# Two transposed inputs of a fused attention and feed-forward kernel, made in another stretch of the program

## The chip, the core and the metric

The kernel runs on one core of a Trainium2 chip. The metric is the time of one execution in microseconds (us), as the device measures it. Profiled executions come with a trace, in which PE is TensorE (matmuls), DVE VectorE, ACT ScalarE, POOL GpSimd and SP SyncE; SP and POOL here mostly issue DMA transfers.

## What is computed

```python
def _attn_ref(q, k, v):                      # (8, 12, 448, 64)
    scores = scale * np.matmul(q, k.transpose(0, 1, 3, 2)) - np.log(S)
    attn = 1.0 / (1.0 + np.exp(-scores))
    return np.matmul(attn, v).astype(np.float32)

def _moe_ref(x, w_in, w_out):                # (3584, 768), (768, 2048), (2048, 768)
    h = x @ w_in
    g = h * (1.0 / (1.0 + np.exp(-h)))
    return (g @ w_out).astype(np.float32)
```

The attention has a sigmoid in place of a softmax, so no row has to be normalised. Its output, with the heads of a token side by side, is the x of the second part: a hidden layer with `h * sigmoid(h)`, and an out layer. Inputs and output are float32; the kernel computes in float16 and adds up in float32.

## The kernel before

**Tiles of the attention.** Four heads of one batch make a *quad*; a batch has three, and there are 24: quads 0 to 2 are batch 0, quads 6 to 8 batch 2, quads 9 to 11 batch 3. The 448 tokens of a quad are cut into seven rounds, so a batch has 21 units `(quad, round)`. For a quad, `load` (L78) brings q and k from memory as float16 rows (`qf`, `kf`, four buffers each) and v (`vf`, three buffers), by transfers that POOL issues. Scores need q and k transposed (`qT`, `kT`, four buffers each). For quads 0 to 5 TensorE transposes them. From quad 6 on it is done by `dma_transpose` (L164): one copy puts the rows in order (`kr` or `qr`, three buffers each), and a transfer from SP's queue transposes them into `kT` or `qT`. `scores` does the scores of one unit, a TensorE stage of four matmuls and a sigmoid on ScalarE. `values` (L232, L243) multiplies a whole quad's attention with v and puts the result into `xT`.

**The second part.** A batch's hidden layer (`moe_h`) has 16 blocks (`h_unit`) of six matmuls, a sigmoid and a product on VectorE. In the out layer, two row blocks make one `out_set`: by a Strassen-like scheme it takes seven products of eight matmuls each (56 in all) in place of eight products. Before, between and after these, VectorE makes sums of the inputs (`S`, L350 to L360) and adds up the products (`osb`, L346); the weights' sums (`T`, L308) are made once, during batch 1's hidden layer and two of them in the first set. The output goes out by SP's queue, from two of the four `osb` buffers for each set. Products, hidden blocks, values and the scores' "single" banks share four PSUM banks (`ps_1`).

**The order.** Everything is issued in the order of the program text, with no scheduler. The second part is one long stream of steps, each a matmul with what belongs to it: hidden layers of batches 0 and 1, sets (0, 0), (0, 2) and (0, 4), hidden layer of batch 2, and so on. A generator (`all_moe`) hands them out. The attention runs beside it in bursts: `burst` issues the scores of two or three units, then `values_if_any`, then `rows_if_any`; then `stretch` takes steps from the stream until they have filled a given time. In `stretch`, when half of it is done, `rows_if_any` is called once more. So behind the first units of batch 2 come steps of set (0, 0), and so on.

**The steps that the change touches.** `after_values` (L496) runs when a quad's values have been issued. It loads v for three quads on and, for quads from 6 on, puts quads into the list `later`, k and q as two entries. `rows_if_any` (L435) takes one entry from the list: it issues the copy on VectorE, the transpose on SP's queue and, behind a q, the load of q and k four quads on, which takes the buffers that have just been copied. Before the change, batch 2's first values (quad 6) put quads 9 and 10 into the list, so four entries are taken by four calls; quads 7 and 8 put in 11 and 12. Quads 6, 7 and 8 are copied by ScalarE within batch 1's hidden layer (`by_h1`), after which POOL waits for the transpose of q of quad 8 (`gate`, L403) and loads quads 10, 11 and 12. Quad 9 is loaded behind quad 5's values. `moe_set` (L407) runs through the steps of a set with an index `i` from 0 to 55 and can put something behind a step; in set (0, 0) these are the last two pieces of the weights' sums, behind 10 and 14.

Of the kernel before, what the change touches and what calls it, by code (L numbers as in the profile page):

```python
# [17 lines left out]
def kernel(  # L18
# [9 lines left out]
    nc = tc.nc  # L28
# [13 lines left out]
    NQB = NQ * B  # L42
# [24 lines left out]
    def new_flat(name, g):  # L67
        flat[name, g] = (p3 if name == "v" else p4).tile(
            [P, 2, NCH, D], F16, tag=f"{name}f", name=f"{name}f"
        )  # L70

    def rows_in(name, g):
        b, iq = divmod(g, NQ)
        return source[name][b, 4 * iq : 4 * iq + 4].rearrange(
            "(i h) (p c) d -> (h p) i (c d)", h=2, c=NCH
        )

    def load(names, g, c0=0, c1=NCH):  # L78
        for name in names:
            if (name, g) not in flat:  # L80
                new_flat(name, g)
            nc.gpsimd.dma_start(  # L82
                flat[name, g][:, :, c0:c1].rearrange("p i c d -> p i (c d)"),
                rows_in(name, g)[:, :, c0 * D : c1 * D],
            )
# [22 lines left out]
    def load_w_in(step):  # L108
        cols = slice(step * DFF // 4, (step + 1) * DFF // 4)
        rows = moe_w_in[:, cols].rearrange("(iq j h d) f -> h j d iq f", j=2, h=2, d=D)  # L110
        for half in range(2):
            for j in range(2):
                nc.gpsimd.dma_start(
                    w_in_sb[j * D : (j + 1) * D, half * NQ : (half + 1) * NQ, cols], rows[half, j]
                )

    def load_w_out(nh, part):
        cols = slice(nh * NO2, (nh + 1) * NO2)
        fcs = slice(part * NFC // 2, (part + 1) * NFC // 2)
        nc.gpsimd.dma_start(  # L120
            w_out_sb[:, fcs, cols],
            moe_w_out[part * DFF // 2 : (part + 1) * DFF // 2, cols].rearrange(
                "(fc p) e -> p fc e", p=P
            ),
        )
# [3 lines left out]
    def new_qkT(g):  # L129
        for name in ("k", "q"):  # L130
            qkT[name, g] = p4.tile([P, NCH, P], F16, tag=f"{name}T", name=f"{name}T")
# [32 lines left out]
    def dma_transpose(g, name, copy):  # L164
        if ("k", g) not in qkT:
            new_qkT(g)
        rows = p3.tile([P, NCH, 2, D], F16, tag=f"{name}r", name=f"{name}r")
        copy(rows, flat[name, g].rearrange("p j c d -> p c j d"))  # L168
        nc.sync.dma_start_transpose(
            out=qkT[name, g], in_=rows.rearrange("p c j d -> p (c j d)")  # L170
        )
# [141 lines left out]
    def block(g):  # L313
        return gTr[:, :, g * P : (g + 1) * P]

    def row_blocks(m, g):
        return [rows_of[2 * m + u // NCH, u % NCH] for u in (2 * g, 2 * g + 1)]
# [89 lines left out]
    def moe_set(m, g):  # L407
        step = out_set(block(g), row_blocks(m, g), block(g + 1), row_blocks(m, g + 1))
        for i, ns in enumerate(step):
            if m % 2 == 0 and g == 2 and i % 8 == 4 and i < 32:  # L410
                fcs = slice(i // 8 * 4, i // 8 * 4 + 4)
                nc.scalar.activation(kept[:, fcs], block(NCH - 1)[:, fcs], AF.Copy)  # L412
            if m == 0 and g == 0 and i in (10, 14):
                next(sums)
            yield ns

    def all_moe():
        for m in range(B // 2):
            yield from moe_h(2 * m)
            if m > 0:  # L420
                yield from moe_set(m, 0)
            yield from moe_h(2 * m + 1)
            if m == 0:
                yield from moe_set(m, 0)
            yield from moe_set(m, 2)
            yield from moe_set(m, 4)
            if m % 2 == 1:
                g = NCH - 1
                yield from out_set(
                    kept, row_blocks(m - 1, g), block(g), row_blocks(m, g), m == B // 2 - 1  # L430
                )

    later = []

    def rows_if_any():  # L435
        if later:
            g, name = later.pop(0)
            dma_transpose(g, name, nc.vector.tensor_copy)
            if name == "q" and g + 4 < NQB and g + 4 > 12:
                load("kq", g + 4)  # L440

    stream = all_moe()
# [2 lines left out]
    def stretch(ns):  # L445
        nonlocal done, due
        due = max(due + ns, done + 0.75 * ns)
        middle = due - ns / 2
        since = 0
        while done < due or hold:  # L450
            step_ns = next(stream, None)
            if step_ns is None:
                break
            done += step_ns * weight
            since += step_ns
            if since > 1300:
                late_sigmoid()
            if done > middle:
                rows_if_any()
                middle = math.inf  # L460
        late_sigmoid()
# [34 lines left out]
    def after_values(g):  # L496
        if g == 0:
            load("v", 3)
            load_w_in(2)
            load_w_in(3)  # L500
        elif g == 1:
            load("v", 4)
            load_w_out(0, 0)
            load_w_out(0, 1)
        elif g == 2:
            load("v", 5)
            load_w_out(1, 0)
            load_w_out(1, 1)
            load("kq", 6)
            load("kq", 7)  # L510
        elif g + 3 < NQB:
            load("v", g + 3)
        if g == 5:
            load("kq", 9)
        if g >= 6:
            for to in (9, 10) if g == 6 else (g + 4,):
                if to < NQB:
                    later.extend(((to, "k"), (to, "q")))

    def values_if_any():  # L520
        if waiting:
            g = waiting.pop(0)
            values(g)
            after_values(g)
# [17 lines left out]
    def rounds(g, end):  # L542
        values(g, end)
        if end == NCH:
            after_values(g)
# [37 lines left out]
    def burst(n, tiles):  # L583

        new = units[n : n + (tiles if not waiting else 2)]
        for i, u in enumerate(new):
            single = i == len(new) - 3
            scores(*u, single_banks() if single else None, len(new) == 3 and i == 2)
        values_if_any()
        rows_if_any()  # L590
        waiting.extend(g for g, ch in new if ch == NCH - 1)
        return len(new)
# [51 lines left out]
```

## Time and profile before

| | us |
|---|---|
| three runs | 382.36, 381.93, 381.32 |
| their median | 381.93 |
| the profiled execution, its own time | 378.82 |
| its span in the trace | 377.1 |
| granted TensorE clock, mean | 0.998 |

The span runs from the first to the last recorded instruction; the execution's own time is 1.7 us more. In the 40 slices of the page, each 9.4 us long, a digit is the busy share in tenths and 9 is 90% or more. The copies that are moved lie in the tenth and eleventh slice:

```profile
PE   7999999999999999999999999999999999999995
DVE  2555646997766466548576557645675457556773
DMA  8999999987999909919599734435062300210333
```

Where these stages lie in the trace: batch 1's hidden layer ends at 76.3 us, set (0, 0) runs from there to 87.7, with bursts of scores within it at 78.5, 82.1 and 85.6 (three units each). The values of quad 6 are at 89.6, those of quad 7 at 97.2 and those of quad 8 at 108.5. The first unit of quad 9 is the last of the three in the burst at 104.5.

In the lines of a timeline below, the columns are the start and the duration in us, the engine, the line of the kernel, the operation, what is written and read, shapes, and how many instructions are merged; in brackets stands how long the engine was idle before and what ended that.

### The profile page before, as it was taken

The numbers are of one execution on the slowest core, as the hardware profiler recorded it, in microseconds if no ns is written. First come the engines' busy times: TensorE is split into PE (matmuls) and PEld (weight loads), VectorE is DVE, ScalarE is ACT, GpSimd is POOL, SyncE is SP. The second block draws the span as 40 slices with busy tenths as digits, with TensorE's granted clock in tenths as the row PEclk, the third lists the DMA queues.
The fourth block names the chain that finished last, engine by engine and source line by source line (L and its number), as shares of the span: only waits on it lengthen the run. The fifth ranks groups of instructions, "written<-read, shape, count | busy, mean of one in ns | idle before, by whom it ended". The sixth has DMA issues, their size and how long they took to land.

```text
span 377.1 us, 7624 instructions
## 1 busy us (share of the span) xinstructions
PE 368.9 (98%) x3081; PEld 189.5 (50%) x3081; DVE 234.0 (62%) x417; ACT 243.3 (65%) x355; POOL 66.1 (18%) x99
## 2 busy tenths in 40 slices
PE   7999999999999999999999999999999999999995
PEld 3544445555554455455555545544555455555663
DVE  2555646997766466548576557645675457556773
ACT  5998885778777776676556676667866685243000
POOL 8565523042412002102120200000000000000000
PEclk9999999999999999999999999999999999999999
DMA  8999999987999909919599734435062300210333
GB/s 137 198 204 204 205 203 203 177 122 153 136 164 223 216 2 120 160 50 108 73 161 193 108 101 75 55 104 75 0 144 41 85 2 2 52 31 2 83 85 83
DMA packets 65698, 42.79 MB, mean 113 GB/s; under 512 B 36096, under 2 KB 62208, under 8 KB 65664
## 3 DMA queue, kind: packets, MB, share of 16 engines
q0 software_dynamic: 27072, 22.58, 41.6%
q1 hardware_dynamic: 38240, 19.44, 28.4%
q8 instruction: 24, 0.39, 0.4%
q10 hardware_dynamic: 352, 0.30, 0.2%
q14 instruction: 10, 0.08, 0.1%
HBM read 45.61 MB, written 11.01 MB: 150 GB/s over the span
## 4 chain that ended last, share of the span: by engine, by line
PE 92%; ACT 6%; issue 1%; DVE 0%; ACTq 0%
PE ph L262 39%; PE po L338 34%; PE psc L196 9%; PE pav L232 8%; ACT attnT L207 5%; PE pw L140 1%; PE ptrq L153 1%; PE ptrk L153 0%; ACT attnT L180 0%; DVE gTr L276 0%; DVE osb L346 0%; ACT kept L412 0%; ACT qT L143 0%; ACT m L353 0%; DVE dummy L476 0%
## 5 line engine op out<-in xcount | busy, mean ns | idle before, releaser
L207 ACT ACTIVATE attnT<-psc,bias_s 128x896 f16<-128x896 f32 (+1 forms) x168 | 138.3, 901 | 45.4 <-PE psc L196 45.2
L262 PE MATMUL ph<-xT,w_in_sb 128*128 128x448 f16 x768 | 151.2, 353 | 0.0
L276 DVE TENSOR_TENSOR gTr<-ph,tsig 128x448 f16<-128x448 f32 x128 | 78.3, 623 | 68.9 <-ACT tsig L274 68.4
L262 PEld LDWEIGHTS <-w_in_sb 128*128 128x128 f16 x768 | 72.8, 98 | 73.6 <-issue 8.2
L274 ACT ACTIVATE tsig<-ph 128x448 f16<-128x448 f32 x128 | 68.4, 549 | 49.1 <-PE ph L262 48.2
L338 PEld LDWEIGHTS <-S 128*128 128x128 f16 x448 | 42.3, 98 | 33.5 <-issue 6.8
L346 DVE SCALAR_TENSOR_TENSOR osb<-po,osb 128x384 f32<-128x384 f32 x70 | 37.6, 554 | 22.4 <-PE po L338 22.1
L196 PE MATMUL psc<-qT,kT 64*64 64x448 f16 x672 | 48.4, 360 | 1.8 <-ACT attnT L207 0.5
L243 DVE TENSOR_SCALAR xT<-pav 128x448 f16<-128x448 f32 x48 | 27.7, 620 | 31.1 <-PE pav L232 31.1
L82 POOL DMA_DIRECT2D vf<-in_v_dram x24 | 17.2, 716 | 166.4 <-PE pav L232 140.3
L338 PE MATMUL po<-T,S 128*128 128x384 f16 x224 | 40.6, 327 | 0.0
L338 PEld LDWEIGHTS <-gTr 128*128 128x128 f16 x304 | 28.7, 98 | 23.5 <-issue 5.4
L338 PE MATMUL po<-w_out_sb,S 128*128 128x384 f16 x224 | 39.9, 326 | 0.0
L232 PE MATMUL pav<-attnT,vf 64*64 64x448 f16 x672 | 38.3, 350 | 0.7 <-DVE gTr L276 0.4
L338 PE MATMUL po<-w_out_sb,gTr 128*128 128x384 f16 x192 | 34.9, 327 | 0.0
L196 PEld LDWEIGHTS <-kT 64*64 64x64 f16 x672 | 16.5, 105 | 29.6 <-issue 25.4
L346 DVE SCALAR_TENSOR_TENSOR osb<-po,m 128x384 f32<-128x384 f32 x42 | 23.2, 553 | 6.2 <-PE po L338 5.1
L232 PEld LDWEIGHTS <-vf 64*64 64x64 f16 x672 | 20.6, 107 | 12.5 <-issue 2.5
L180 ACT ACTIVATE attnT<-psc,bias_s 128x896 f16<-128x896 f32 x26 | 26.6, 1022 | 0.0
L353 ACT ACTIVATE m<-po 128x384 f32<-128x384 f32 x14 | 6.9, 495 | 23.7 <-PE po L338 23.7
L338 PE MATMUL po<-T,gTr 128*128 128x384 f16 x112 | 21.4, 326 | 0.0
L82 POOL DMA_DIRECT2D kf<-in_k_dram x25 | 18.1, 723 | 16.6 <-DVE kr L168 10.3
(43 smaller groups left out, 155.0 us busy)
## 6 DMA issues: line engine op xcount, KB each, us to landing
out_dram<-osb SPq DMA_DIRECT2D x54, 192.0 KB, 2.9
vf<-in_v_dram POOLq DMA_DIRECT2D x24, 224.0 KB, 5.3
kf<-in_k_dram POOLq DMA_DIRECT2D x23, 224.0 KB, 6.5
qf<-in_q_dram POOLq DMA_DIRECT2D x23, 224.0 KB, 7.4
w_in_sb<-in_moe_w_in_dram POOLq DMA_DIRECT2D x16, 192.0 KB, 8.2
w_out_sb<-in_moe_w_out_dram POOLq DMA_DIRECT2D x4, 768.0 KB, 15.4
kT<-kr SPq DMA_TRANSPOSE x18, 6.8
qT<-qr SPq DMA_TRANSPOSE x18, 6.9
```

Of the source, the lines that this page charges most:

```text
L82: nc.gpsimd.dma_start(flat[name, g][:, :, c0:c1].rearrange("p i c d -> p i (c d)"), rows_in(name, g)[:, :, c0 * D : c1 * D],)
L180: nc.scalar.activation(to, psc, AF.Sigmoid, bias=bias_s, scale=QKSCALE)
L196: nc.tensor.matmul(banks[j][own, :S], qkT["k", g][rows, ch, own], qkT["q", g][rows, :, own], start=True, stop=True,)
L207: nc.scalar.activation(to, psc, AF.Sigmoid, bias=bias_s, scale=QKSCALE)
L232: nc.tensor.matmul(pav[half][j * D : (j + 1) * D, :S], flat["v", g][own, j, ch, :], at[own, j, :], start=(ch == 0), stop=(ch == NCH - 1),)
L243: nc.vector.tensor_scalar_mul(xT[b][:, half * NQ + iq, :], pav[half][:, :S], SX)
L262: nc.tensor.matmul(ph[:, :S], w_in_sb[:, cc, fc * P : (fc + 1) * P], xT[b][:, cc, :], start=(at == 0), stop=(at == NCC - 1),)
L274: nc.scalar.activation(tsig, ph[:, :S], AF.Sigmoid, bias=0.0, scale=ISX)
L276: nc.vector.tensor_mul(gTr[:, fc, (b % 2) * S : (b % 2) * S + S], ph[:, :S], tsig)
L338: nc.tensor.matmul(po[:, :NO2], a[:, fc, :], w[:, fc, :], start=(fc == 0), stop=(fc == NHC - 1))
L346: nc.vector.scalar_tensor_tensor(out=o, in0=po, scalar=sign, in1=x, op0=ALU.mult, op1=ALU.add)
L353: nc.scalar.activation(m1, po, AF.Copy, scale=ISX)
```

## The change

```diff
@@ moe_set
             if m == 0 and g == 0 and i in (10, 14):
                 next(sums)
+            if m == 0 and g == 0 and i in (24, 40):
+                dma_transpose(9, "k" if i == 24 else "q", nc.vector.tensor_copy)
+                if i == 40:
+                    load("kq", 13)
             yield ns
@@ rows_if_any
             dma_transpose(g, name, nc.vector.tensor_copy)
-            if name == "q" and g + 4 < NQB and g + 4 > 12:
+            if name == "q" and g + 4 < NQB:
                 load("kq", g + 4)
@@ after_values
         if g >= 6:
-            for to in (9, 10) if g == 6 else (g + 4,):
-                if to < NQB:
-                    later.extend(((to, "k"), (to, "q")))
+            if g + 4 < NQB:
+                later.extend(((g + 4, "k"), (g + 4, "q")))
```

Quad 9's copies and transposes leave the list `later` and are issued in set (0, 0), k behind step 24 and q behind step 40; the load of quad 13 comes right behind the latter. Quad 6's values put only quad 10 into the list, so 10's entries are taken two calls earlier, and quad 14's load is issued with them. The second hunk drops a condition that is true for every quad which comes by there. Matmuls, sigmoids and their order stay as they are, and so does the number of copies, transposes and loads.

## The prediction

> **What bounds the kernel now.** I read the page first (busy times, slices, chain), then the waits of TensorE, then the timeline of each engine from 74 to 112 us, which holds the place the copies go to and the place they leave, then the DMA view there.
>
> ```profile
> span 377.1 us, 7624 instructions
> PE 368.9 (98%) x3081; PEld 189.5 (50%) x3081; DVE 234.0 (62%) x417; ACT 243.3 (65%) x355; POOL 66.1 (18%) x99
> PE 92%; ACT 6%; issue 1%; DVE 0%; ACTq 0%
> ```
>
> TensorE is busy for 98% of the span and the chain of waits runs through it for 92%. Idle are 377.1 - 368.9 = 8.2 us; the slices put most of it in the first (7 tenths) and the last (5 tenths). The list of TensorE's waits holds five, 3.2 us in all:
>
> ```profile
> PE pw L140 <- DVE bias_s L477: 1.5, 1, 1.5
> PE psc L196 <- ACT attnT L207: 0.5, 1, 0.5
> PE psc L196 <- ACT qT L143: 0.5, 1, 0.5
> PE pav L232 <- DVE gTr L276: 0.4, 1, 0.4
> PE pav L232 <- ACT attnT L207: 0.3, 1, 0.3
> ```
>
> By the chain all of them lie before 50 us, and between 57.5 and 137 us TensorE idles for 0.01 us. So in this execution nothing in reach of the change can be made shorter: an edit pays only if it ends a wait that this execution does not show, and costs only if it makes one.
>
> **What is moved, on VectorE.** The copies of quad 9 go into the first set (76.3 to 87.7 us). I count the set's 56 matmuls: 14 lie before the scores at 78.56, 17 before those at 82.12, 17 before those at 85.68. Step 24 is the first matmul of the fourth product, at about 80.9; step 40 is the first of the sixth, at about 84.2. VectorE takes its work in order, so the copy of k stands behind the addition of the third product (82.14) and ahead of the first of the fourth (83.12):
>
> ```profile
> 82.14 0.55 DVE L346 SCALAR_TENSOR_TENSOR osb<-po,m 128x384 f32<-128x384 f32 x1
> 83.12 0.56 DVE L346 SCALAR_TENSOR_TENSOR osb<-po,osb 128x384 f32<-128x384 f32 x1 [0.42 <-PE po L338]
> 83.59 0.55 DVE L346 SCALAR_TENSOR_TENSOR osb<-po,m 128x384 f32<-128x384 f32 x1
> 84.42 0.56 DVE L346 SCALAR_TENSOR_TENSOR osb<-po,osb 128x384 f32<-128x384 f32 x1 [0.28 <-PE po L338]
> 85.72 1.02 DVE L346 SCALAR_TENSOR_TENSOR osb<-po,osb 128x384 f32<-128x384 f32 x2 [0.74 <-PE po L338]
> ...
> 92.17 0.61 DVE L168 COPY kr<-kf 128x896 f16<-128x896 f16 x1
> 92.70 0.61 DVE L168 COPY qr<-qf 128x896 f16<-128x896 f16 x1
> 93.23 0.55 DVE L346 SCALAR_TENSOR_TENSOR osb<-po,m 128x384 f32<-128x384 f32 x1
> ```
>
> The idle time is in brackets. A copy takes 0.61 us and the next instruction starts 0.53 after it (92.17, 92.70, 93.23); an addition costs 0.46 in the same sense (83.59 - 83.12 = 0.47). The copy of k runs from about 82.60 to 83.13, and the addition that came at 83.12 comes at 83.13: cost 0.01 us on VectorE. The copy of q stands behind the fifth product's addition (84.42), runs from 84.88 to 85.41, and the next comes at 85.72 as before. Both are hidden in waits for TensorE of 0.42 and 0.74 us. If that cover is gone, the two delay VectorE by 2 x 0.53 = 1.06 us; late next is a PSUM bank that the next product, or the single banks of the scores at 85.61, must have.
>
> **Behind batch 2's first values** the list then holds 10 alone: its copies take the places of 9's at 92.17 and 92.70, and those at 94.29 and 95.28 vanish. The additions behind these start up to 0.5 us earlier; TensorE waited for none of them (no such row among its waits), so on this trace the gain is 0.00 us. The input of 10 is in place for it: qf of quad 10 is the load issued at 78.53, landing after 5.1 us.
>
> **The queues.** POOL's six loads for 10 to 12 are issued from 77.82 to 82.61; the two for 13, which waited for 9's copies and came at 93.09 and 93.80, now come at about 83.5 and 85.8, and nothing stands behind them until v of quad 9 at 91.41. Those for 14 move from 95.20 and 96.19 to about 93.1 and 93.8. SP's queue:
>
> ```profile
> 86.30 3.21 SPq L331 DMA_DIRECT2D out_dram<-osb  x4
> 92.85 1.23 SPq L169 DMA_TRANSPOSE kT<-kr  x1
> 94.17 1.39 SPq L169 DMA_TRANSPOSE qT<-qr  x1
> 95.67 4.22 SPq L169 DMA_TRANSPOSE kT<-kr  x1
> 99.98 4.09 SPq L169 DMA_TRANSPOSE qT<-qr  x1
> 104.17 4.12 SPq L169 DMA_TRANSPOSE kT<-kr  x1
> ```
>
> The transposes of 9 go ahead of the set's four stores, at about 83.2 and 85.5. At 1.2 to 1.4 us each the stores start up to about 0.6 late; at 4.2 each (the rows from 95.67 on) they start at 91.6 instead of 86.30 and end at 94.8. Their tiles are written again only by the third set, at 106.28. With 5 us to land, the longest median of the stores in this stretch, that leaves over 6 us: cost nothing. The transposes of 10 then follow by about 95 at the latest.
>
> **The one thing that is tight.** The first scores of quad 9 are the third tile of the burst at 104.50:
>
> ```profile
> qT<-qr SPq DMA_TRANSPOSE x1, 10.3
> ...
> 104.50 0.76 PE L196 MATMUL psc<-qT,kT 64*64 64x448 f16 x12
> ```
>
> The first row is the transpose of q for quad 9, issued at 94.17; the last number is its time to landing. It lands at 94.17 + 10.3 = 104.47. The tile's four weight loads start by 104.7, so it had about 0.25 us to spare, by chance. Transposes here take very different times: 6.5 us for k of 9, 13.3 and 13.0 for k and q of 10, against 2.9 at the least in this trace, because they share the 16 engines with POOL's loads for 13, 14 and v. (The Trainium skill's page "DMA: Bandwidth & Descriptors", in "Queues, rings and completion order", says that each DMA engine takes the queues with work in turn, packet by packet. The rows agree: 13.3 us in the jam, 2.9 outside it; by the page a transpose's landing hangs on the loads beside it.) In an execution in which that one transpose takes 0.3 us longer, TensorE stands still in front of the tile, and as it has no slack anywhere, the end moves by what it waits. The price, from the nearest rows: nothing at 10.3 us or less; 94.17 + 13.3 - 104.7 = 2.8 us at the length of the next transpose. After the change this tile's transposes start 9 us earlier and even at 13.3 us land before 99, 6 us early; those of 10 land by about 108, needed at 118.10.
>
> **The sum.** For the profiled execution: 0.0 us, span 377 as before. But this execution's own time was 378.82 (1.7 around its span), and the three runs gave 381.32 to 382.36, median 381.93: 3.1 us more, and 1.04 apart. The trace cannot say what the 3.1 us are. A late qT of quad 9, worth 0 to 2.8 us, is one thing that fits. I take 1.5, about the middle, since the rows on both sides (10.3 and 13.3) are equally near. Forecast 381.93 - 1.5 = **380.4 us**; its own range is 379.0 to 380.7.
>
> **The rivals.** (1) *The transfer is hidden anyway.* The profiled execution speaks for it: no wait, and nothing else in reach. Then the 3.1 us are a matter of the runs that the change doesn't touch: 381.9 us, give or take 0.6. Against it is only that 0.25 us is little beside landings that differ by 7 us.
>
> (2) *VectorE becomes late in the first set.* It has no idle time from 73.7 to 82.7 us, and the copy of k stands right behind that stretch. The place is the fourth product's additions, whose bank TensorE needs between 84.22 (the sixth product's start) and 85.61 (the next single banks); they end at 84.15 now. It decides once they end after that, 0.1 to 1.5 us later. Price: the two copies, 1.06 us, and for each one issue of a POOL load (0.72 us) if the two engines hinder each other, as the copy of k starts when the last of those loads has just been issued (81.89 to 82.61): 1.06 + 1.44 = 2.5 us at most, 383.7 with some 0.7 of it covered by the waits that VectorE has there. Against it: four waits for TensorE in this set, 0.28 to 1.07 us, each of which takes up delay. (The Trainium skill's page "SBUF — State Buffer", in "Who interferes with whom", has a rule against the change: a fast copy of VectorE and an instruction of GpSimd block each other for their whole length. No row here shows it; by it either copy could wait, or the loads for 12 and 13 be late, and these are needed at 111 us and later.)
>
> (3) *The edit is empty*: 9's input not there at step 24. Its loads were issued at 60.82 and 62.01 and took 9.1 and 9.5 us, so they landed by 71.5; this I give no chance.
>
> **How the numbers follow.** Less than 0.3%, 1.15 us, is about what a measurement here can't tell from no change. Forecast 0.46, rival (1) 0.39, rival (2) 0.15. These are the chances of faster, same and slower: the forecast's bulk lies below 380.78, rival (1) stays above it, and (2) goes past 383.08. The range 378.9 to 382.9 holds the forecast's lower end (all of the 2.8 us and a little of spread), all of rival (1), and leaves out most of (2) and a little below.
>
> **What would show it.** In the trace after: copies at about 82.6 and 84.9 with VectorE's additions where they were, two copies left at 92.2 and 92.7, none until 99.8; transposes of 9 issued at 83 and 85.5 and landed before 99; POOL's loads for 13 at 83.5 and 85.8; TensorE's waits as before, span 377 within 0.4. Wrong on the mechanism would be a new wait of scores or products between 82 and 92 us (rival 2); wrong on the size, if timed runs stay at 381.9 while the trace has all of the above (rival 1). A transpose of 9 put back at its old place with the loads beside it taken away would tell (1) from the forecast.

## The result and the profile after

| | before | after |
|---|---|---|
| runs compared | 22 | 22 |
| median, us | 380.28 | 378.68 |
| lowest to highest, us | 378.57 to 382.87 | 377.98 to 379.04 |
| ratio after / before | | 0.9952, 95% interval 0.9937 to 0.9968 |
| profiled execution, own time / span, us | 378.82 / 377.1 | 379.04 / 377.3 |

The change makes the kernel 0.5% faster, and its times lie much closer together: 20 of the 22 runs before are slower than the slowest run after. The two profiled executions show nothing of it, since the one before happens to be among the fastest.

The first lines of the page and of the chain, and of TensorE's waits, after the change:

```profile
span 377.3 us, 7624 instructions
PE 368.2 (98%) x3081; PEld 188.7 (50%) x3081; DVE 234.3 (62%) x417; ACT 242.9 (64%) x355; POOL 66.3 (18%) x99
PE 90%; ACT 5%; DMA 2%; issue 1%; POOL 1%; DVE 0%; POOLq 0%; ACTq 0%
```

```profile
PE pw L140 <- DVE bias_s L481: 1.5, 1, 1.5
PE ptrq L153 <- DMA qf<-in_q_dram: 0.9, 1, 0.9
PE psc L196 <- ACT qT L143: 0.6, 1, 0.6
```

There is no new wait in the changed stretch. The one for `qf` and the chain's "DMA 2%" are from the start of the kernel, where TensorE's transposes wait for a load; other executions, of the kernel before as well, show it with 0.2 to 0.8 us. VectorE's timeline where quad 9's copies now are and, in the last two lines, where they were and quad 10's now are:

```profile
82.40 0.55 DVE L346 SCALAR_TENSOR_TENSOR osb<-po,m 128x384 f32<-128x384 f32 x1
82.87 0.61 DVE L168 COPY kr<-kf 128x896 f16<-128x896 f16 x1
83.40 0.55 DVE L346 SCALAR_TENSOR_TENSOR osb<-po,osb 128x384 f32<-128x384 f32 x1
83.86 0.55 DVE L346 SCALAR_TENSOR_TENSOR osb<-po,m 128x384 f32<-128x384 f32 x1
84.69 0.56 DVE L346 SCALAR_TENSOR_TENSOR osb<-po,osb 128x384 f32<-128x384 f32 x1 [0.28 <-PE po L338]
85.16 0.61 DVE L168 COPY qr<-qf 128x896 f16<-128x896 f16 x1
85.99 1.02 DVE L346 SCALAR_TENSOR_TENSOR osb<-po,osb 128x384 f32<-128x384 f32 x2 [0.22 <-PE po L338]
...
92.44 0.61 DVE L168 COPY kr<-kf 128x896 f16<-128x896 f16 x1
92.97 0.61 DVE L168 COPY qr<-qf 128x896 f16<-128x896 f16 x1
```

This execution started 0.27 us later (its first scores of batch 2 come at 78.76 in place of 78.49). With that taken off, every addition stands where it was to 0.01 us: the first copy fills the wait of 0.42 us, the second takes 0.52 of the 0.74. And the transposes, from SP's timeline, with q of quad 9's row of the DMA view:

```profile
83.54 1.23 SPq L169 DMA_TRANSPOSE kT<-kr  x1
85.80 1.88 SPq L169 DMA_TRANSPOSE qT<-qr  x1
87.77 2.93 SPq L331 DMA_DIRECT2D out_dram<-osb  x4
93.12 1.39 SPq L169 DMA_TRANSPOSE kT<-kr  x1
```

```profile
qT<-qr SPq DMA_TRANSPOSE x1, 10.0
```

It lands at 85.80 + 10.0 = 95.8, and the scores of quad 9 start at about 105.0: 9 us to spare where there was a quarter of one. The transfer itself is no quicker than before (10.0 us against 10.3); it only starts earlier.

### The profile page after: what moved, and what is told of

Same layout as the page of the kernel before. It is cut to its first block, busy times and chain, and to the rows that moved or that the text cites. A ratio compares the mean times of both kernels' runs of the same rounds, so it can differ in the third digit from the quotient of the medians.

```text
span 377.3 us, 7624 instructions
## 1 busy us (share of the span) xinstructions
PE 368.2 (98%) x3081; PEld 188.7 (50%) x3081; DVE 234.3 (62%) x417; ACT 242.9 (64%) x355; POOL 66.3 (18%) x99
## 4 chain that ended last, share of the span: by engine, by line
PE 90%; ACT 5%; DMA 2%; issue 1%; POOL 1%; DVE 0%; POOLq 0%; ACTq 0%
PE ph L262 39%; PE po L338 34%; PE psc L196 9%; PE pav L232 8%; ACT attnT L207 4%; DMA qf<-in_q_dram 2%; POOL kf L82 1%; PE ptrq L153 0%; PE ptrk L153 0%; ACT attnT L180 0%; DVE gTr L276 0%; DVE osb L346 0%; ACT kept L412 0%; ACT m L353 0%; ACT tsig L274 0%
```

## The experiments

Each edit is against the kernel before, unless it says otherwise. The theory is that q of quad 9 lands too late for its first scores in most executions; the rivals are VectorE's relief behind batch 2's first values, and the earlier loads.

**The kernel before, profiled twice more.** What was expected:

> The kernel before, unchanged, for another profile: three of four runs of it were over 379.1 us. Late-transpose theory: in such an execution the trace shows one new wait of TensorE, scores for qT at about 105 us, of about the length that the execution is over 378.6 (less what a lower clock behind the wait takes), and q of quad 9 landing that much after 104.7. Rival: a slower execution without that wait.

> As the run before it: the kernel before once more, since one in four of its executions has no wait to show.

The first took 378.57 us and had no wait; q of quad 9 was issued at 93.89 and took 9.7 us, landing at 103.6. The second took 380.63. Its row among TensorE's waits, the time to landing of q of quad 9 (issued at 94.24), and TensorE's timeline there:

```profile
PE psc L196 <- DMA qT<-qr: 1.5, 1, 1.5
```

```profile
qT<-qr SPq DMA_TRANSPOSE x1, 12.3
```

```profile
104.57 0.57 PE L196 MATMUL psc<-qT,kT 64*64 64x448 f16 x8
106.68 0.38 PE L196 MATMUL psc<-qT,kT 64*64 64x448 f16 x4 [1.54 <-DMA qT<-qr]
107.00 0.99 PE L338 MATMUL po<-w_out_sb,gTr 128*128 128x384 f16 x5
```

In the trace shown before the change, the burst was twelve matmuls in one piece. Here it is broken behind the eighth: units 61 and 62 have their inputs, unit 63 waits until 94.24 + 12.3 = 106.54, and TensorE goes on 0.14 us later. The wait, 1.54 us, is three quarters of the 2.06 us between the two executions. Of the other 0.52 us, 0.35 is there ahead of the burst, which begins at 104.57 against 104.22.

**Only quad 9's copies and transposes moved** (its entries stay in the list and do only the load of 13, so the loads and quad 10 keep their places in the program):

```diff
+            if m == 0 and g == 0 and i in (24, 40):
+                dma_transpose(9, "k" if i == 24 else "q", nc.vector.tensor_copy)
...
-            dma_transpose(g, name, nc.vector.tensor_copy)
+            if g != 9:
+                dma_transpose(g, name, nc.vector.tensor_copy)
```

> Only quad 9's copies and transposes are moved into the first set; the loads of 13 and 14 and the transposes of 10 stay where they were. Late-transpose theory: the whole gain is here, 378.7 us +- 0.4, with runs as close together as after the change (within 1.1 us), where before spreads over 4 us; q of quad 9 lands before 99 us, needed at 104.7. Rival that the gain comes from the earlier loads or from quad 10: as before, median about 380.3. Rival that it comes from VectorE being relieved behind batch 2's first values: a part of the gain, 379 to 380, since 10's copies stay there.

378.77 us (378.05 to 378.81), ratio 0.9965 (0.9945 to 0.9984) to a median of 379.94 for before. q of quad 9 was issued at 85.53 and landed after 4.2 us. So the whole gain is in these lines; neither the load of 13 in the first set nor quad 10's earlier turn is needed for it.

**Copies alone moved**, the transposes left at the old place:

```diff
+            if m == 0 and g == 0 and i in (24, 40):
+                copy_rows(9, "k" if i == 24 else "q", nc.vector.tensor_copy)
...
-        copy(rows, flat[name, g].rearrange("p j c d -> p c j d"))
+        if (name, g) not in row_of:
+            copy_rows(g, name, copy)
+        else:
+            copy(row_of[name, g][:, 0, 0, :2], flat[name, g][:, 0, 0, :2])
```

> VectorE's copies of quad 9 are moved as in the change, but the transposes, loads and quad 10 stay at their old places (VectorE rewrites two elements of each row there, for which the transposes wait). Late-transpose theory: as before, median about 380.3 with runs from 378.6 to 382.9. Rival that VectorE's relief is the gain: 378.7.

379.14 us (378.53 to 382.28), ratio 0.9987 (0.9963 to 1.0011). The median is 0.8 us below before's, but the interval holds no difference and excludes the changed kernel's 0.9952 only narrowly, so the times alone are weak. The spread is that of the kernel before, and the profiled execution, at 382.28 us, shows the wait with VectorE relieved (the row is below). The lower median may have its cause in the edit itself: with only two elements left to copy there, q's transpose is issued 10.73 us ahead of the burst, against 10.33 in all three traces of the kernel before. No run tests that.

```profile
PE psc L204 <- DMA qT<-qr: 2.7, 1, 2.7
```

**VectorE's old work put back into the changed kernel**, as copies into a spare tile; first beside quad 10's own copies, then in the third and fourth call, where 10's were (diff of the latter, against the changed kernel):

```diff
+            if g == 6:
+                later.extend(((None, "k"), (None, "q")))
...
+            if g is None:
+                spare = p2.tile([P, NCH, 2, D], F16, tag="spare", name="spare")
+                nc.vector.tensor_copy(spare, flat[name, 11].rearrange("p j c d -> p c j d"))
+                return
```

> The changed kernel with two more copies of the same size on VectorE, into a spare tile, beside quad 10's copies, so that VectorE has as much to do behind batch 2's first values as before the change. Late-transpose theory: 378.7 +- 0.4, as after the change. Rival that VectorE's relief there is the gain: 380.3.

> The changed kernel with two idle copies of the same size in the third and fourth call behind batch 2's first values, just where VectorE had quad 10's before, so that VectorE has before's work at before's places. Late-transpose theory: 378.7 +- 0.3, and no wait of a product for VectorE (the earlier run with idle copies beside 10's own had one of 0.5 us, since all four stood ahead of the second product's addition). Rival of VectorE's relief: 379.5 to 380.

The first gave 379.09 us (378.25 to 379.35), 0.4 above the changed kernel, though not timed side by side with it: all four copies stood ahead of the second product's addition, and TensorE waited for VectorE once, 0.5 us. With the copies at their old places it is 378.76 us (377.94 to 378.98), and that wait is gone. VectorE's relief is worth nothing that can be seen here; where a copy stands among the additions made one wait of half a microsecond.

**The load beside the transposes taken away**, with all copies and transposes at their old places: quads 13 and 14 loaded behind 11's transposes, then 14 alone, then, as the edit was meant, 13 alone (diff of the first):

```diff
-            if name == "q" and g + 4 < NQB and g + 4 > 12:
-                load("kq", g + 4)
+            if name == "q" and g + 4 < NQB and g > 10:
+                for to in (13, 14, 15) if g == 11 else (g + 4,):
+                    load("kq", to)
```

> Everything as before, with copies and transposes of 9 and 10 at their old places; only the loads of 13 and 14 are issued later, behind the transposes of 11 together with the load of 15, so that they no longer share the DMA engines with 9's transposes. Late-transpose theory: q of quad 9 is issued at about 94 and lands by 101 (6.5 us or less in place of 10.3 and more), so that no run waits: 378.7 +- 0.4. Rival of VectorE or of the copies' place: nothing of theirs is changed, 380.3. If the trouble is SP's queue and not the loads, 380.3 as well.

> As before the change, but quad 14's load alone is issued later, behind 11's transposes. It was issued just behind q of 9's transpose (95.2 and 96.2 against 94.2). Late-transpose theory with DMA engines that share: fewer and shorter waits, q of 9 landing in 6 to 9 us, median 378.8 to 379.4. If only what is issued ahead of the transpose matters: as before, about 380.

> As before the change, but quad 13's load alone is issued later, behind 11's transposes; 14's stays at about 95. 13's load was issued at 93.1 and 93.8, ahead of q of 9's transpose. If either load taken away is enough (the engines share, and with less beside it the transpose lands before 104.7): 378.4 to 378.9 and no wait, as with 14 alone taken away. If it is the load behind the transpose that holds it up and not the one ahead: 379.5 to 380.

| loads taken away | median (range), us | ratio to before (95%) | q of quad 9 in the trace: issued, to landing, landed |
|---|---|---|---|
| 13 and 14 | 378.71 (378.24 to 378.84) | 0.9970 (0.9951 to 0.9988) | 93.63, 3.3, 96.9 |
| 14 | 378.45 (378.06 to 378.98) | 0.9949 (0.9925 to 0.9974) | 94.14, 9.1, 103.2 |
| 13 (but see below) | 378.79 (378.19 to 378.95) | 0.9973 (0.9957 to 0.9989) | 93.69, 9.3, 103.0 |

The last run did not do what was meant, and its expectation (14's load stays at about 95) did not hold. With 13's load out of the way, 14's is the next to ask for buffers, gets those that quad 9's copies free, and comes where 13's was, ahead of q's transpose at 93.69. POOL's timeline:

```profile
92.61 0.71 POOL L82 DMA_DIRECT2D kf<-in_k_dram  x1 [0.95 <-DVE kr L168]
93.31 0.72 POOL L82 DMA_DIRECT2D qf<-in_q_dram  x1
```

The next load of a q or k comes at 99.29. With 14's load taken away these times are 93.06, 93.77 and 99.74, so the two runs have the same traffic, 0.45 us apart: the last row is a repetition of the one above it, and the load ahead of the transpose was never taken away alone.

The first two rows are the strongest test: nothing that TensorE, VectorE or SP does is moved, only transfers whose data nobody needs before 120 us, and the gain is there in full; with 14 alone gone it is more than was expected (378.8 to 379.4). With both loads gone, the transpose that took 9.7 to 12.3 us takes 3.3. The load that is issued behind the transpose, gone alone, is enough: what is issued later still shares the engines with it. Traces at the new place say the same of k of quad 9. With quad 13's loads right behind it (at 83.78 and 86.07, it at 83.54) it took 10.2 us in the changed kernel, and 9.6 and 7.6 in the two runs with idle copies; without them, in the run with only quad 9's moved, 5.7. (The Trainium skill's page "DMA: Bandwidth & Descriptors", in "Queues, rings and completion order", says that a DMA engine takes the queues with work in turn, a packet at a time. These rows agree: a load issued behind the transpose, on another queue, holds it up.) With the one load gone the traces leave 1.3 and 1.5 us to spare, with both 7; the changed kernel has 9.

**The same transposes later still**: quad 10 ahead of quad 9 in the list, so that 9's take the places of 10's (13 is still the first quad to be loaded, now behind 10's q).

```diff
-            for to in (9, 10) if g == 6 else (g + 4,):
+            for to in (10, 9) if g == 6 else (g + 4,):
```

> As before, but quad 10 stands ahead of quad 9 in the list, so that 9's transposes take the places of 10's, issued at 95.7 and 100.0, which landed at 109 and 113. Late-transpose theory: scores of quad 9, due at 104.7, wait for the landing, 4 to 9 us: 383 to 388 us, and the trace shows TensorE waiting for qT there. Rival that the landing isn't what matters: 380.3.

388.13 us (four runs, 385.69 to 388.58), ratio 1.0206 (1.0166 to 1.0245). q of quad 9 was issued at 100.22 and took 12.5 us, to 112.7; TensorE's row in the timeline:

```profile
112.88 0.59 PE L196 MATMUL psc<-qT,kT 64*64 64x448 f16 x4 [7.78 <-DMA qT<-qr]
```

The wait is 7.8 us and the time 9.4 above the changed kernel's. The end moves by the wait, and by something more, which is told below.

## Why the prediction was right and where it failed

**The mechanism is as forecast.** The trace's 0.25 us between the landing of q of quad 9 and its first use was the place. The transposes beside loads do land at very different times, the wait moves the end, and a transpose issued 9 us earlier lands in time, though it is no shorter: shown by the trace with the wait, by the two one-part edits, and by the loads taken away. That most executions come too late is inferred from the times: of three traces of the kernel before, one has the wait, but 20 of 22 timed runs were slower than any run after, and no run with quad 9's part alone moved, or with both loads taken away, took more than 378.84 us.

**VectorE and the queues** went as worked out. Copies were forecast at 82.6 and 84.9, the transposes at 83.2 and 85.5 and POOL's loads of 13 at 83.5 and 85.8; they came at 82.87 and 85.16, 83.54 and 85.80, 83.78 and 86.07, 0.26 to 0.34 us later, about the 0.27 us by which this execution was later. The four stores started at 87.77, 1.2 us late with that taken off, between the forecast's two cases, and TensorE's waits show nothing of it. The sum of 0.0 us for the profiled execution holds (377.1 and 377.3).

**The step that failed is the last line of the sum, "381.93 - 1.5 = 380.4", and with it the range from 378.9.** The measured 378.68 lies below it. The term for the wait, 1.5 us, was mis-sized for what it was taken from. Over 22 runs of the kernel before, the medians differ by 380.28 - 378.68 = 1.60 us, so 1.5 is right for a typical execution. But the three runs that were given, 381.32 to 382.36, lie in the upper third of those 22. Their median is 381.93 - 378.68 = 3.25 us above the changed kernel, more than the 2.8 that I took as the most; they have no trace, so that all of this is the wait and what follows it is inferred. The typical price was subtracted from an untypical start. And there was a better way to the number: if the theory is right, the changed kernel has no such wait, and its time is that of an execution without one. One was at hand, the profiled one, with 378.82 us. Taking half of the 3.1 us as "something else" was a hedge between the forecast and its rival, not a price, and that its 1.5 is near the typical 1.60 is in part luck: it was the middle of a range whose upper end was too low.

**The bound of 2.8 us was too low** for a second reason: it counted the wait alone. The slowest runs of before, 382.87 and, in the later comparisons, 383.41, are 4.2 and 4.7 us over the changed kernel's median. What a longer wait costs beyond itself is in the last section.

**The rivals.** That the transfer is hidden anyway described the profiled execution and no more than a few of the others. That VectorE becomes late in the first set did not happen: two of the four waits for TensorE there took up both copies. Its mechanism is real elsewhere, as the idle copies ahead of an addition showed, with a wait of 0.5 us.

## What to carry to other kernels

A trace in which nothing waits can still be the trace of a lucky execution. When timed runs are slower than the profiled one and lie apart by more than the usual, look in the trace for transfers that land a fraction of a microsecond before their first use, and compare with how much the landing times of their kind differ. When such a transfer is the cause, the time after mending it is that of the execution that did not wait; and it can be mended from either side, by starting the transfer earlier or by moving transfers off it that nobody needs yet. When a transfer is moved away, look in the trace for what came into its place: here the next load took its buffers and its time.

## What the runs showed of the hardware

**A wait can cost more than its length.** In two traces TensorE's granted clock halved during the wait, and in a third, with a shorter wait, it did not. Busy times by stretch in the execution with copies alone moved, whose wait ran from 104.40 to 107.08 (columns: stretch, length, busy time and instructions of each engine, granted clock, DMA share, GB/s):

```profile
104.40:106.50 2.10, 0.00 (x0) 0.00 (x0) 0.23 (x1) 1.97 (x3) 0.00 (x0) 1.00 1.31 176
106.50:109.60 3.10, 2.52 (x11) 1.16 (x12) 0.12 (x1) 1.01 (x1) 0.00 (x0) 0.50 1.25 186
109.60:112.00 2.40, 2.40 (x23) 1.25 (x24) 1.59 (x3) 0.00 (x0) 0.00 (x0) 0.93 2.10 149
```

The clock falls to 0.50 at 106.5, 2.1 us into the wait, and stays there through the second stretch. The 0.93 of the third is 0.34 us at half clock out of 2.40, so it is back at about 109.9, 2.9 us after TensorE has its data: 3.4 us at half clock. From the first matmul of unit 63 to the first of quad 8's values it is 111.99 - 107.08 = 4.91 us, against 110.27 - 106.68 = 3.59 behind the wait of 1.54 us, in which the clock stayed at 1.00: 1.3 us more. Behind the wait of 7.78 us, which began at 105.10, the clock was low from 109.6 (4.5 us into it; 0.80 between 109 and 110) to 116.4 (0.89 between 116 and 118), 6.8 us, and the same work took 118.14 - 112.88 = 5.26 us, 1.7 more. So in these traces a wait of 1.5 us cost 1.5, and one of 2.7 cost 4.0. (The Trainium skill's page "TensorE: Matmul & The Clock Gate", in "What's actually happening", says that the clock goes by activity in windows of about 3.4 us that run freely. That the fall comes 2.1 us into one wait and 4.5 into another, and that the clock stays low for 3.4 and 6.8 us, agrees with free-running windows; that the first needed no whole idle window of that length does not agree with the table there, which asks for one.)

**Beside loads the issue itself can take longer.** With both loads taken away, the four transposes of quads 9 and 10 took 1.2 us each to issue on SP. With the loads there, the last two of the four took 3.6 to 6.1 in the three traces of the kernel before and the two with copies alone moved or quad 10 ahead (4.22 for k of quad 10 in the trace before the change). SP issues in order, so a late transpose also holds up the next: in the run with quad 10 ahead of quad 9, q of quad 9 had been copied by 95.9 and was issued at 100.22, when the one ahead of it was through.
